# Second-layer sums of one batch: from VectorE adds in SBUF to accumulating transfers into DRAM

## The chip, the cores and the metric

One core of a Trainium2 chip. The metric is the device time of one execution in microseconds; of several runs the median is taken. The core has TensorE (PE: matrix products, with results in PSUM banks), VectorE (DVE), ScalarE (ACT), GpSimd (POOL) and SyncE (SP, which issues most transfers). The engines run side by side, each in its own order, and wait for each other through semaphores.

## The reference

Sigmoid attention, a gated two-matrix block with a shift of one position, and then the block that the change is in. Four batches of S = 448 rows, D = 768 columns, hidden width 3072, all float32. Cut to the part that matters:

```
X = fft(fft(x, axis=1), axis=2)
u = x + real(X)
un = (u - mean(u)) / sqrt(var(u) + 1e-06)
ch = max(un @ w_ch1, 0) @ w_ch2
return u + ch
```

## The kernel before, in words

Every float32 product is done as three PE products of halves: a value is split into `hi` (a rounding cast) and `lo` (the rest), and hi·hi, hi·lo, lo·hi are added in one PSUM bank. A matmul here is 128x128 weights by 448 columns.

The last block keeps `u` transposed in DRAM as `u_d[b]`, six tiles of 128x448 for each batch b. The hidden width is cut into 12 groups g of 256. For batches 0 and 1 `ffn1(g, b)` makes two hidden tiles (18 matmuls each) and `ffn2(g, b)` makes six tiles f2_g_b_e, each of which has to be added to the residual. Batch 0 takes each group by itself (6 matmuls a tile); batch 1 takes g = 0 and g = 1 alone and then two groups at once (12 matmuls a tile), so it has 7 rounds of six tiles. From g = 2 on the order on PE is f1(g,0), f1(g,1), f2(g,0), f1(g+1,0), f1(g+1,1), f2(g+1,0), f2(g+1,1). Batches 2 and 3 come afterwards, in `pair1` and `ffn2(g, 2)`, `ffn2(g, 3)`, with the weights `v2`. Below, f1(g,b) and f2(g,b) are these steps on PE.

The residual sum lives in SBUF: `load_acc(b)` loads `u_d[b]` into a tile `acc[b]` (tag `x2`, three buffers), `out_done` has DVE add each PSUM tile to it, and at the last group the tile goes to `out`. A PSUM bank is free again when its add is done; `bank2` has five of them for these tiles.

Beside this runs `convert`: each weight block w1 or w2 of group g, half i, comes from DRAM as 64-bit numbers (768 KB, by SP) and is turned into float32 on DVE in four steps, then split:

```
yield o.ts(bits, top, 3, 0x3FFFFFF8, ALU.logical_shift_left, ALU.bitwise_and)
yield o.stt(bits, top, 0xC0000000, bits, ALU.bitwise_and, ALU.bitwise_or)
yield o.stt(bits, low, 29, bits, ALU.logical_shift_right, ALU.bitwise_or)
yield o.stt(w, w, TINY, bits.bitcast(F32), ALU.is_ge, ALU.mult)
```

`finish` then has ACT cast `w` to `hi` and POOL subtract it (`lo`, line 215). PE can use the block after that. `prepare_rows` also runs here: DVE and ACT turn batches 2 and 3 into the operands of `pair1`, in a third `x2` tile, `acc2`.

The order of instructions on every engine is written out before the run by the class `Order`: generators such as `convert` and `out_done` yield a time, a planner with a clock of its own (`o.now`, with a cost for each operation) resumes whichever is next, and what it emits becomes the engine's queue. So a change of planned costs moves instructions of other steps against each other.

Of the kernel before, what the change touches and what calls it, by code (L numbers as in the profile page):

```python
# [12 lines left out]
F32 = mybir.dt.float32  # L13
# [3 lines left out]
ALU = mybir.AluOpType  # L17
# [3 lines left out]
B, H, S, DH = 4, 12, 448, 64  # L21
# [4 lines left out]
KD = D // 128  # L26
FF2 = 4 * D
GF = 256
NG = FF2 // GF
# [80 lines left out]
class Order:  # L110
# [126 lines left out]
    def dma(self, out, src, eng=None):  # L237
        (eng or self.nc.sync).dma_start(out, src)
        b = 512 * self.size(out) * (4)
        start = max(self.now + 2.0, self.free.get("dma", 0.0))  # L240
        self.free["dma"] = start + b / 4.0 / 280e3
        return self.free["dma"] + 0.2


def build(tc, ap):
    nc = tc.nc
    V, G = nc.vector, nc.gpsimd
    o = Order(nc)
    est = ExitStack()

    def pool(stack, name, bufs=1, side="left", space=None):
        if space is not None:
            return stack.enter_context(tc.tile_pool(name=name, bufs=bufs, space=space))
        return stack.enter_context(tc.tile_pool(name=name, bufs=bufs, side=side, reuse_waits="tile"))
# [65 lines left out]
    u_d = [dram.tile([128, KD, S], F32, name=f"u_d{b}") for b in range(B)]  # L320
# [182 lines left out]
    for f in range(NF + KD):  # L503
        if f < NF:
            src, hl, key = ap["w_k"][f], [w[:, f].rearrange(flat) for w in (wkh, wkl)], ("wk", f)
        else:
            src, hl, key = ap["w_r"][f - NF], [w.rearrange(flat) for w in wr_t[f - NF]], ("wr", f - NF)
# [148 lines left out]
    np_ = pool(s_r, "norm", 1, "right")  # L656
# [5 lines left out]
    for i, n in enumerate((113, 112, 112, 111)):  # L662
        c = fp.tile([128, 2, TW], F32R, name=f"ct{i}")
# [264 lines left out]
    def load_rs(b, tag):  # L928
        yield from o.need(("rs_d", b))
        rs_t[b] = np_.tile([128, S], F32, tag=tag, name=f"rsb_{b}", bufs=1)  # L930
        o.at["rs", b] = o.dma(rs_t[b], rs_d[b].to_broadcast([128, S]))
# [7 lines left out]
    def load_early(nm, g, pl):  # L939

        ts = w_t[nm, g] = [
            [pl.tile([128, D], F32R, tag=nm + t, name=f"{nm}{t}{g}_{i}", bufs=2) for t in "hl"] for i in range(2)
        ]
        for i in range(2):
            for c, t in enumerate(ts[i]):
                t = o.dma(t.bitcast(F32), w0_d[nm, g][i][:, c])
            o.at.update(((nm, g, i, c), t) for c in range(3))
# [9 lines left out]
    wpa = pool(s_l, "wpa", 2, "left")  # L957
    hp = pool(s_l, "hp", 2, "left")
    wpb1 = pool(s_l, "wpb1", 2, "left")
    acc, h_t = {}, {}  # L960

    def load_acc(b, *keys):

        yield from o.need(*keys, *(("u_d", b, i) for i in range(3)))
        acc[b] = np_.tile([128, KD, S], F32, tag="x2", name=f"acc{b}", bufs=3)
        o.at["acc", b] = o.dma(acc[b], u_d[b])
        yield o.now

    def parts_of(out, src, key, eng):

        yield o.act(out[0], src)
        o.at[key] = t = o.sub(eng, out[1], src, out[0])
        yield t
# [98 lines left out]

    def prepare_rows():

        yield from o.need(*(("centre", b) for b in range(2, B)), ("acc", 1))
        yield from load_rs(2, "rsb")
        yield from load_rs(3, "sum_u")
        wk = np_.tile([128, KD, S], F32, tag="x2", name="acc2", bufs=3)
        yield from o.need(("rs", 2), ("rs", 3))

        def put(nm, d, src):
            if nm not in LATE:
                t = t_t[nm, d] = tp.tile([128, 2, S], F32R, name=f"{nm}_{d}")
                yield from parts_of((t[:, 0], t[:, 1]), src, ("t", nm, d), V)
                return
            t = np_.tile([128, 2, S], F32R, tag="sq", name=f"{nm}_{d}", bufs=1)
            yield from parts_of((t[:, 0], t[:, 1]), src, ("row", nm, d), V)
            o.at["t_d", nm, d] = t = o.dma(t_d[nm, d], t.bitcast(F32))
            yield t + 2.0

        for d in range(3):
            b11, b21, b12, b22 = (wk[:, i] for i in range(4))
            for x, b, e in ((b11, 2, d), (b12, 3, d), (b21, 2, d + 3), (b22, 3, d + 3)):
                yield o.dma(x, c_d[b][:, e])
                yield o.tt(V, x, x, rs_t[b], ALU.mult) + 1.0
            yield from put("B11", d, b11)
            yield o.tt(V, b11, b12, b11, ALU.subtract) + 1.0
            yield from put("T1", d, b11)
            yield o.tt(V, b12, b22, b12, ALU.subtract) + 1.0
            yield from put("T3", d, b12)  # L1100
            yield from put("B22", d, b22)
            yield o.tt(V, b22, b22, b11, ALU.subtract) + 1.0
            yield from put("T2", d, b22)
            yield from put("B21", d, b21)
            yield o.tt(V, b21, b21, b22, ALU.subtract) + 1.0
            yield from put("T4", d, b21)
        acc[2] = wk
        o.at["acc", 2] = o.dma(wk, u_d[2])
# [9 lines left out]
    def hidden(g, b, i, src):  # L1118
# [2 lines left out]
        o.at["h", g, b, i] = o.stt(t[:, 1], src, 0.0, t[:, 0].bitcast(F32), ALU.max, ALU.subtract)  # L1121
        yield o.at["h", g, b, i]

    def out_done(g, b, e, ps):
        yield from o.need(("acc", b))
        a = acc[b][:, e]
        t = o.tt(V, a, a, ps, ALU.add)
        yield t
        if g == NG - 1:
            o.at["out", b, e] = o.dma(ap["out"][e, :, S * b : S * b + S], a) + 2.0  # L1130
            yield o.now

    def network():
# [14 lines left out]
        def ffn2(g, b):  # L1148
            nm = "w2" if b < 2 else "v2"
            gi = [(c, i) for c in ((g - 1, g) if b == 1 and g > 1 else (g,)) for i in range(2)]  # L1150
            yield from o.need(*(("h", c, b, i) for c, i in gi))
            hs = [h_t.pop((c, b, i)) for c, i in gi]
            yield from o.need(*((nm, c, i, 2) for c, i in gi), ("acc", b))
            ws = [w_t[nm, c][i] for c, i in gi]
            for e in range(KD):
                es = slice(128 * e, 128 * e + 128)

                def pair(i, es=es):
                    return ws[i][0][:, es], ws[i][1][:, es], hs[i][:, 0], hs[i][:, 1]

                yield from o.tile(partial(bank2, f"f2_{g}_{b}_{e}"), len(gi), pair, partial(out_done, g, b, e))
            while len(o.feed) > 3:
                yield o.now + 0.1

# [61 lines left out]
        for n, t in enumerate(first):  # L1226
            order.append((ffn2, "w2", t))
            order += [(ffn1, "w1", t) for t in (first + [(2, 0), (2, 1)])[n + 2 : n + 3]]
        for g in range(2, NG, 2):
            order += [(ffn1, "w1", (g, 0)), (ffn1, "w1", (g, 1))] if g > 2 else []  # L1230
            order += [(ffn2, "w2", (g, 0))]
            order += [(ffn1, "w1", (g + 1, 0)), (ffn1, "w1", (g + 1, 1)), (ffn2, "w2", (g + 1, 0)), (ffn2, "w2", (g + 1, 1))]
# [17 lines left out]
    def first_loads():  # L1250
        yield from o.issued(("un", 1, 2))
        load_early("w2", 0, wpa)
        yield from o.issued(("un", 1, 5))
        o.spawn(load_acc(0, ("centre", 1)))
        o.spawn(load_acc(1, ("acc", 0), ("centre", 2)))
        yield o.now + 4.0
        load_early("w1", 1, wpb1)

    o.spawn(first_loads())
    o.spawn(network())  # L1260
    o.run(("four", B - 1))
# [10 lines left out]
    o.spawn(convert())  # L1272
    o.spawn(second_group())
    o.spawn(prepare_rows())
    o.run("converted")
    s_w.close()
# [69 lines left out]
```

## Time and profile before

| | us |
|---|---|
| median of 3 runs | 1229.59 (1227.28 to 1230.06) |
| profiled execution | 1231.31 |
| its span in the trace | 1229.5 |
| PE busy | 1216.5 |
| DVE busy | 907.4 |
| ACT busy | 479.1 |
| POOL busy | 135.3 |

The profiled execution is one run by itself; 1.8 us of its time lie outside the span. Busy times are sums over the span and overlap. The part that the change touches goes from about 562 us (the first f1 and f2) to 896 us (the first `pair1`).

### The profile page before, as it was taken

The page shows a single profiled execution, that of the slowest core. Times are in us where ns is not written, and L with a number is a line of the kernel's source. Part 1 is how long each engine was busy: PE and PEld are TensorE (multiplying, and loading weights), DVE is VectorE, ACT ScalarE, POOL GpSimd, SP SyncE. Part 2 cuts the span into 40 slices and gives each one's busy share as a digit, 9 for nine tenths or more (in the row PEclk, how much of TensorE's full clock was granted, in tenths as well). Part 3 has the DMA queues.
Part 4 walks back from the last instruction along what each step waited for, and adds up shares of the span by engine and source line. Part 5 has one row for each costly group of instructions (what it writes and reads, how often), then busy time and mean ns, then how long its engine had stood idle before and what let it go on. Part 6 is the DMA issues. An engine that isn't in the chain of part 4 may idle for free. (4 is left out here: it accounts for less than half of the span.)

```text
span 1229.5 us, 16416 instructions
## 1 busy us (share of the span) xinstructions
PE 1216.5 (99%) x6142; PEld 1050.5 (85%) x6142; DVE 907.4 (74%) x1425; ACT 479.1 (39%) x864; POOL 135.3 (11%) x97
## 2 busy tenths in 40 slices
PE   8999999999999999999989999999999999999998
PEld 3467766789999998999979999999999999999998
DVE  5776887656853669797999999897566776776654
ACT  5867767766530122142333333332132332322220
POOL 0000000000000000000232232222021111121110
PEclk9999999999999999999999999999999999999999
DMA  6656669666948446396555555555842112121102
GB/s 219 223 169 229 213 239 339 237 243 231 320 158 259 169 165 218 113 316 227 184 202 212 184 200 203 201 186 188 314 141 78 52 54 75 52 66 63 52 1 90
DMA packets 77296, 217.82 MB, mean 177 GB/s; under 512 B 9312, under 2 KB 31776, under 8 KB 76576
## 3 DMA queue, kind: packets, MB, share of 16 engines
q1 hardware_dynamic: 76544, 214.37, 50.3%
q0 software_dynamic: 672, 2.40, 0.6%
q8 instruction: 48, 0.79, 0.3%
q14 instruction: 32, 0.26, 0.1%
HBM read 143.84 MB, written 72.90 MB: 176 GB/s over the span
## 5 line engine op out<-in xcount | busy, mean ns | idle before, releaser
L215 DVE TENSOR_TENSOR acc<-acc,f 128x448 f32<-128x448 f32 x258 | 156.6, 616 | 66.4 <-PE f L180 63.8
L180 PE MATMUL f<-h,w2h 128*128 128x448 f32 x576 | 165.6, 368 | 3.6 <-DVE acc L215 3.6
L180 PE MATMUL f<-un,w1h 128*128 128x448 f32 x576 | 166.2, 368 | 0.0
L180 PE MATMUL f<-h,v2h 128*128 128x448 f32 x576 | 163.6, 365 | 0.0
L180 PEld LDWEIGHTS f<-h,w2h 128*128 128x128 f32 x576 | 107.8, 188 | 14.9 <-DVE acc L215 4.8
L234 ACT ACTIVATE sg<-sc,bias_s 128x448 f32<-128x448 f32 x168 | 95.0, 651 | 60.7 <-PE sc L180 60.7
L180 PEld LDWEIGHTS f<-un,w1h 128*128 128x128 f32 x576 | 108.2, 188 | 10.4 <-issue 0.4
L180 PEld LDWEIGHTS f<-h,v2h 128*128 128x128 f32 x576 | 108.2, 188 | 8.5
L180 PE MATMUL v<-k,wvh 128*128 128x448 f32 x384 | 113.4, 370 | 0.8 <-DMA k<-k_d 0.7
L180 PE MATMUL f<-un,w1l 128*128 128x448 f32 x288 | 105.9, 368 | 0.0
L180 PE MATMUL f<-h,w2l 128*128 128x448 f32 x288 | 105.9, 368 | 0.0
L180 PE MATMUL f<-h,v2l 128*128 128x448 f32 x288 | 105.2, 365 | 0.0
L223 DVE SCALAR_TENSOR_TENSOR w_bits<-w_raw,w_bits 128x768 uint32<-128x768 uint32 x80 | 99.9, 1248 | 1.0
L180 PE MATMUL av<-sg,v 128*64 128x448 f32 (+1 forms) x336 | 81.1, 549 | 0.0
L180 PEld LDWEIGHTS v<-k,wvh 128*128 128x128 f32 x384 | 71.6, 188 | 8.1 <-DMA k<-k_d 2.4
L215 POOL TENSOR_TENSOR v2l<-v,v2h 128x768 fp32r<-128x768 f32 x24 | 46.8, 1970 | 275.0 <-ACT v2h L232 275.0
L215 POOL TENSOR_TENSOR w1l<-w,w1h 128x768 fp32r<-128x768 f32 x20 | 41.2, 2062 | 300.6 <-ACT w1h L232 295.5
L180 PE MATMUL v<-k,wvl 128*128 128x448 f32 x192 | 70.8, 369 | 0.0
L180 PE MATMUL k<-xkh,wkh 128*128 128x448 f32 x192 | 70.7, 368 | 0.0
L180 PE MATMUL k<-xkl,wkh 128*128 128x448 f32 x192 | 70.4, 367 | 0.0
L180 PE MATMUL k<-xkh,wkl 128*128 128x448 f32 x192 | 70.3, 366 | 0.0
L180 PEld LDWEIGHTS av<-sg,v 128*64 128x64 f32 (+1 forms) x336 | 27.9, 144 | 42.5 <-issue 35.9
(175 smaller groups left out, 2356.7 us busy)
## 6 DMA issues: line engine op xcount, KB each, us to landing
w_raw<-in_w SPq DMA_DIRECT2D x40, 768.0 KB, 4.5
w_d<-w SPq DMA_DIRECT2D x40, 384.0 KB, 2.6
k_d<-kp SPq DMA_DIRECT2D x32, 448.0 KB, 2.8
k<-k_d SPq DMA_DIRECT2D x32, 448.0 KB, 6.3
a<-w_d SPq DMA_DIRECT2D x24, 384.0 KB, 3.5
v<-w_d SPq DMA_DIRECT2D x24, 384.0 KB, 3.0
k<-in_k SPq DMA_DIRECT2D x24, 256.0 KB, 5.5
v<-in_v SPq DMA_DIRECT2D x24, 256.0 KB, 3.0
```

The costliest lines, as they stand in the source:

```text
L180: self.nc.tensor.matmul(out, lhs, rhs, start=start, stop=stop, skip_group_check=skip)
L215: eng.tensor_tensor(out, a, c, op=op)
L223: self.nc.vector.scalar_tensor_tensor(out, a, scalar, c, op0=op0, op1=op1)
L234: self.nc.scalar.activation(out, a, fn, **kw)
```

## The change

It concerns batch 1 alone. In place of `acc[1]` there is a tile `stage` of the same size that holds no sums. `out_added` has ACT copy each PSUM tile into `stage[:, e]`; then a transfer issued by GpSimd adds it to `u_d[1][:, e]` in DRAM. After the last group the sum goes from DRAM to `out`, issued by SP. The planner gets a cost for the new step (`add_to`); `prepare_rows` waits for `stage` in the place of `acc[1]`.

```diff
+    def add_to(self, out, src):
+        g = self.nc.gpsimd
+        g.dma_start(out, src, accum_op=ALU.add)
+        t = self.spend(g, 1.2)
+        took = 512 * self.size(out) * 2 / 280e3
+        self.free["dma"] = max(self.now, self.free.get("dma", 0.0)) + took
+        return max(t + 2.0, self.free["dma"]) + took + 0.2
...
     def prepare_rows():
-        yield from o.need(*(("centre", b) for b in range(2, B)), ("acc", 1))
+        yield from o.need(*(("centre", b) for b in range(2, B)), "stage")
...
+    def make_stage():
+        yield from o.need(("acc", 0), ("centre", 2), *(("u_d", 1, i) for i in range(3)))
+        stage[0] = np_.tile([128, KD, S], F32, tag="x2", name="stage", bufs=3)
+        o.at["stage"] = o.now
+        yield o.now
+
+    def out_added(g, e, ps):
+        a = stage[0][:, e]
+        yield o.act(a, ps)
+        o.at["added", g, e] = o.add_to(u_d[1][:, e], a)
+        if g == NG - 1:
+            yield o.at["added", g, e]
+            o.at["out", 1, e] = o.dma(ap["out"][e, :, S : 2 * S], u_d[1][:, e]) + 2.0
+        yield o.now
...
-            yield from o.need(*((nm, c, i, 2) for c, i in gi), ("acc", b))
+            yield from o.need(*((nm, c, i, 2) for c, i in gi), ("acc", b) if b != 1 else "stage")
...
-                yield from o.tile(partial(bank2, f"f2_{g}_{b}_{e}"), len(gi), pair, partial(out_done, g, b, e))
+                done = partial(out_done, g, b, e) if b != 1 else partial(out_added, g, e)
+                yield from o.tile(partial(bank2, f"f2_{g}_{b}_{e}"), len(gi), pair, done)
...
-        o.spawn(load_acc(1, ("acc", 0), ("centre", 2)))
+        o.spawn(make_stage())
```

PE keeps its order of f1 and f2 tiles. On DVE 42 adds go, and what is left stands in another order against PE's tiles. First place: DVE's queue around the conversion of w1_3_1, the weights of the second tile of f1(3,0) and f1(3,1). Before (`f1_2_1_0` is a tile of f1(2,1), `f2_2_0_0` the first of f2(2,0)):

```order
L215 TENSOR_TENSOR acc1_5716<-acc1_5716,f2_1_1_5_6110 128x448
L227 TENSOR_SCALAR w1_3_1_bits_6128<-w1_3_1_raw_6074 128x768
L215 TENSOR_TENSOR acc2_6039<-acc2_6039,rsb_2_5908 128x448
L223 SCALAR_TENSOR_TENSOR w1_3_1_bits_6128<-w1_3_1_raw_6074,w1_3_1_bits_6128 128x768 x2
L223 SCALAR_TENSOR_TENSOR h_2_1_0_6153<-f1_2_1_0_6118,h_2_1_0_6153 128x448
L223 SCALAR_TENSOR_TENSOR w1_3_1_6127<-w1_3_1_6127,w1_3_1_bits_6128 128x768
L227 TENSOR_SCALAR w2_3_0_bits_6182<-w2_3_0_raw_6125 128x768
L223 SCALAR_TENSOR_TENSOR w2_3_0_bits_6182<-w2_3_0_raw_6125,w2_3_0_bits_6182 128x768
L215 TENSOR_TENSOR acc2_6039<-acc2_6039,rsb_3_6037 128x448
L215 TENSOR_TENSOR acc0_5505<-acc0_5505,f2_2_0_0_6186 128x448
```

And in the changed kernel, where `f2_2_0_5` is the last tile of f2(2,0):

```order
L215 TENSOR_TENSOR acc0_5505<-acc0_5505,f2_2_0_3_6199 128x448
L215 TENSOR_TENSOR acc0_5505<-acc0_5505,f2_2_0_4_6210 128x448
L215 TENSOR_TENSOR acc0_5505<-acc0_5505,f2_2_0_5_6218 128x448
L227 TENSOR_SCALAR w1_3_1_bits_6230<-w1_3_1_raw_6149 128x768
L223 SCALAR_TENSOR_TENSOR w1_3_1_bits_6230<-w1_3_1_raw_6149,w1_3_1_bits_6230 128x768
L215 TENSOR_TENSOR acc2_6066<-acc2_6066,rsb_3_6064 128x448
L223 SCALAR_TENSOR_TENSOR w1_3_1_bits_6230<-w1_3_1_raw_6149,w1_3_1_bits_6230 128x768
L223 SCALAR_TENSOR_TENSOR w1_3_1_6229<-w1_3_1_6229,w1_3_1_bits_6230 128x768
L227 TENSOR_SCALAR w2_3_0_bits_6247<-w2_3_0_raw_6227 128x768
L223 SCALAR_TENSOR_TENSOR w2_3_0_bits_6247<-w2_3_0_raw_6227,w2_3_0_bits_6247 128x768
```

The final step of w1_3_1 stood ahead of the add of the first tile of f2(2,0); now the whole conversion stands behind the add of its last tile.

Second place: DVE's queue around w2_4_1, the second half of the weights of f2(4,0) (`f1_4_0` and `f1_4_1` are the tiles of f1(4,0) and f1(4,1), which PE does right before). Before:

```order
L223 SCALAR_TENSOR_TENSOR h_4_0_0_6593<-f1_4_0_0_6557,h_4_0_0_6593 128x448
L227 TENSOR_SCALAR w2_4_1_bits_6613<-w2_4_1_raw_6559 128x768
L223 SCALAR_TENSOR_TENSOR w2_4_1_bits_6613<-w2_4_1_raw_6559,w2_4_1_bits_6613 128x768 x2
L223 SCALAR_TENSOR_TENSOR h_4_0_1_6627<-f1_4_0_1_6590,h_4_0_1_6627 128x448
L223 SCALAR_TENSOR_TENSOR w2_4_1_6612<-w2_4_1_6612,w2_4_1_bits_6613 128x768
L215 TENSOR_TENSOR acc2_6039<-acc2_6039 128x448
L223 SCALAR_TENSOR_TENSOR h_4_1_0_6658<-f1_4_1_0_6625,h_4_1_0_6658 128x448
```

And in the changed kernel:

```order
L223 SCALAR_TENSOR_TENSOR h_4_0_0_6608<-f1_4_0_0_6573,h_4_0_0_6608 128x448
L223 SCALAR_TENSOR_TENSOR w2_4_0_6590<-w2_4_0_6590,w2_4_0_bits_6591 128x768
L223 SCALAR_TENSOR_TENSOR h_4_0_1_6634<-f1_4_0_1_6606,h_4_0_1_6634 128x448
L223 SCALAR_TENSOR_TENSOR h_4_1_0_6659<-f1_4_1_0_6632,h_4_1_0_6659 128x448
L227 TENSOR_SCALAR w2_4_1_bits_6673<-w2_4_1_raw_6588 128x768
L223 SCALAR_TENSOR_TENSOR w2_4_1_bits_6673<-w2_4_1_raw_6588,w2_4_1_bits_6673 128x768 x2
L223 SCALAR_TENSOR_TENSOR h_4_1_1_6687<-f1_4_1_1_6657,h_4_1_1_6687 128x448
L223 SCALAR_TENSOR_TENSOR w2_4_1_6672<-w2_4_1_6672,w2_4_1_bits_6673 128x768
```

The final step of w2_4_1 stood ahead of `h_4_1_0`, the first hidden tile of f1(4,1); now it stands behind `h_4_1_1`, the last one.

Third place: POOL's queue from its `ct` loads on, where before there were only the subtracts (`w1l2_0` is the lo half of w1, g = 2, i = 0). In the changed kernel:

```order
L672 DMA ct3_3908<-in_ct 111x452
L246 DMA u_d1_140<-stage_5716 128x448 x6
L215 ISA
L215 TENSOR_TENSOR w1l2_0_5720<-w1_2_0_5788,w1h2_0_5719 128x768
L215 TENSOR_TENSOR w1l2_1_5722<-w1_2_1_5896,w1h2_1_5721 128x768
L246 DMA u_d1_140<-stage_5716 128x448 x2
L215 TENSOR_TENSOR w2l2_0_5938<-w2_2_0_6027,w2h2_0_5937 128x768
L246 DMA u_d1_140<-stage_5716 128x448 x4
L215 TENSOR_TENSOR w2l2_1_5940<-w2_2_1_6076,w2h2_1_5939 128x768
L215 TENSOR_TENSOR w1l3_0_6119<-w1_3_0_6151,w1h3_0_6118 128x768
L215 TENSOR_TENSOR w1l3_1_6121<-w1_3_1_6229,w1h3_1_6120 128x768
```

The issues of the accumulates stand between the subtracts of the weights, up to six in a row.

## Rows read from the trace of the kernel before

**Rows 1.** The page, part 1: busy time, share of span, instructions.

```profile
PE 1216.5 (99%) x6142; PEld 1050.5 (85%) x6142; DVE 907.4 (74%) x1425; ACT 479.1 (39%) x864; POOL 135.3 (11%) x97
```

**Rows 2.** Waits of PE: total us, times, longest us.

```profile
PE f L180 <- DVE acc L215: 3.6, 2, 2.0
```

**Rows 3.** Timeline of PE: start us, us, what, [idle before <-releaser].

```profile
594.92 0.57 PE L180 MATMUL f<-h,w2h 128*128 128x448 f32 x2
...
609.52 0.57 PE L180 MATMUL f<-h,w2h 128*128 128x448 f32 x2
...
617.73 0.67 PE L180 MATMUL f<-h,w2h 128*128 128x448 f32 x2 [1.97 <-DVE acc L215]
...
619.05 0.56 PE L180 MATMUL f<-un,w1h 128*128 128x448 f32 x2
...
633.63 0.57 PE L180 MATMUL f<-h,w2h 128*128 128x448 f32 x2
...
641.48 0.68 PE L180 MATMUL f<-h,w2h 128*128 128x448 f32 x2 [1.60 <-DVE acc L215]
```

**Rows 4.** Windows: busy us of each engine, granted clock, DMA share, GB/s.

```profile
core 0: us, PE busy (x) PEld busy (x) DVE busy (x) ACT busy (x) POOL busy (x), PEclk, DMA share, GB/s
640.00:900.00 260.00, 258.52 (x1251) 234.79 (x1252) 224.21 (x288) 80.55 (x122) 65.35 (x33) 1.00 0.59 211
600.00:650.00 50.00, 46.43 (x226) 42.04 (x225) 49.67 (x61) 15.01 (x23) 13.90 (x7) 1.00 0.54 192
850.00:900.00 50.00, 50.00 (x245) 45.53 (x244) 26.29 (x42) 10.28 (x18) 5.92 (x4) 1.00 0.66 245
```

**Rows 5.** The chain that ended last: start us, us, what.

```profile
641.48 254.62 PE f L180 x1230
...
956.72 14.60 PE f L180 x72
```

**Rows 6.** Timeline of DVE, 612 to 618 us.

```profile
612.44 0.95 DVE L223 SCALAR_TENSOR_TENSOR w<-w,w_bits 128x768 f32<-128x768 f32 x1
613.43 0.56 DVE L227 TENSOR_SCALAR w_bits<-w_raw 128x768 uint32<-128x768 uint32 x1
614.02 0.96 DVE L223 SCALAR_TENSOR_TENSOR w_bits<-w_raw,w_bits 128x768 uint32<-128x768 uint32 x1
614.90 2.25 DVE L215 TENSOR_TENSOR acc<-acc,rsb 128x448 f32<-128x448 f32 x1
617.07 0.61 DVE L215 TENSOR_TENSOR acc<-acc,f 128x448 f32<-128x448 f32 x1
617.60 0.61 DVE L223 SCALAR_TENSOR_TENSOR h<-f,h 128x448 fp32r<-128x448 f32 x1
```

**Rows 7.** Timelines of ACT and POOL, 599 to 617 us.

```profile
613.43 0.84 ACT L232 CAST w1h<-w 128x768 fp32r<-128x768 f32 x1 [4.94 <-DVE w L223]
...
599.92 1.85 POOL L215 TENSOR_TENSOR w2l<-w,w2h 128x768 fp32r<-128x768 f32 x1 [2.81 <-ACT w2h L232]
...
614.35 2.31 POOL L215 TENSOR_TENSOR w1l<-w,w1h 128x768 fp32r<-128x768 f32 x1 [5.17 <-ACT w1h L232]
```

**Rows 8.** Timelines of PE and DVE at the end of f1(1,1).

```profile
578.70 0.57 PE L180 MATMUL f<-h,w2h 128*128 128x448 f32 x2
...
579.47 0.62 DVE L223 SCALAR_TENSOR_TENSOR h<-f,h 128x448 fp32r<-128x448 f32 x1 [0.71 <-ACT h L234]
```

**Rows 9.** Groups of instructions: shapes, count, busy us, mean ns.

```profile
L232 ACT COPY x<-av 128x448 f32<-128x448 f32 x24 | 12.8, 532 | 6.1 <-issue 3.9 <-PE av L180 2.2
...
L664 POOL DMA_DIRECT2D ct<-in_ct x4 | 2.2, 573 | 0.0
```

**Rows 10.** DMA issues: KB each, median us to landing; the software queue.

```profile
q0 software_dynamic: 672, 2.40, 0.6%
...
w_raw<-in_w SPq DMA_DIRECT2D x40, 768.0 KB, 4.5
...
out<-acc SPq DMA_DIRECT2D x24, 224.0 KB, 2.0
...
cd<-in_cd POOLq DMA_DIRECT2D x1, 1548.0 KB, 13.0
```

More of the change, by code (lines that the diff above doesn't have):

```diff
@@ L959, in build @@
     wpb1 = pool(s_l, "wpb1", 2, "left")
-    acc, h_t = {}, {}
+    acc, h_t, stage = {}, {}, {}
     def load_acc(b, *keys):
```

## The prediction

> **What bounds the kernel now.** I read the page's first part, then what PE waited for, then the chain that ended last, and last the timelines of the few places where PE stopped. PE is busy 1216.5 us of a span of 1229.5, DVE 907.4, ACT 479.1 and POOL 135.3 [rows 1]; so TensorE's own work sets the time, and a change to the other engines counts only where PE is made to wait or is let off a wait. In the part of the program that the change touches PE waited for DVE's `acc` adds twice, 3.6 us together [rows 2]: 1.97 us ahead of the last tiles of f2(2,0) and 1.60 us ahead of the last tile of f2(3,0) [rows 3]. There a PSUM bank was wanted whose tile DVE had not yet added. DVE is the reason: from 600 to 650 us it is busy 49.67 of 50 us [rows 4], so what is queued on it in that stretch comes out late. Near the end of the stage (850 to 900) it has half its time free [rows 4].
>
> PE also has two paces with the same granted clock (1.00 in every window, the 2.4 GHz level [rows 4]). In the chain 1230 matmuls from 641.48 take 254.62 us, 207.0 ns each, and 72 matmuls at 956.72 take 14.60 us, 202.8 ns each [rows 5]. The slow pace began at the wait at 641.48; the stretch to the end of the stage costs 1230 × 4.2 ns = 5.2 us more than the fast pace would. The trace does not say why it began.
>
> **The change, removed.** 42 adds of f2(g,1) leave DVE. In a run of adds one takes 0.53 us start to start (617.07 to 617.60 [rows 6]), so 42 × 0.53 = 22.3 us leave the engine that was full. That removes both waits of [rows 2]: the f2(2,0) one came because six adds of f2(1,1) were done late, and the f2(3,0) one behind the same backlog. Gain 1.97 + 1.60 = 3.57 us. The load of acc1 goes too; nothing waited for it.
>
> **Added, hidden.** 42 ACT copies of 128x448: the like copy takes 532 ns [rows 9], 22.3 us in all, on an engine that is busy 80.55 of 260 us in the stage [rows 4]. 42 DMA issues on POOL: those of `ct` took 573 ns [rows 9], 24.1 us on an engine busy 65.35 of 260 [rows 4]. Cover: at most six issues stand between two subtracts in POOL's order, 3.4 us, and POOL stood idle 2.81 and 5.17 us ahead of its subtracts, waiting for ACT's cast [rows 7]; without that cover each issue would make a subtract 0.57 us later. The transfers: no accumulate of 224 KB stands in the trace. From below, the plain 224 KB store of `out` lands in 2.0 us; from above, the 1548 KB load that POOL issued in 13.0 [rows 10]. I take some 6 us, between them, since it reads and writes DRAM and its issuer is the latter's. A slot of `stage` is used again no earlier than the next f2(g,1), 47 us later for f2(1,1) to f2(3,1) (594.92 to behind 641.48 [rows 3]), so neither bound makes the copy wait. The last step, DRAM to DRAM, starts after 896 us with 330 us of PE work left: nothing. Traffic: 42 × 2 × 0.229 MB = 19.3 MB more; the stage moved 211 GB/s at a DMA share of 0.59 [rows 4], so 100% would be 358 GB/s, and 19.3 MB are 54 us of it over some 330 us, a share of about 0.75 in place of 0.59. The raw weight loads (4.5 us [rows 10]) should stay ahead; the other case is a rival.
>
> **Moved.** The order of DVE is written out again by the planner's clock, and the conversions of three weights now stand later against PE's tiles. The chain behind each final step `w<-w,w_bits` is a cast on ACT and a subtract on POOL: from 612.44 + 0.95 = 613.39 to 614.35 + 2.31 = 616.66, that is 3.27 us, or with the faster subtract of 1.85 us 2.81 [rows 6, 7]. PE wants the subtract's result at the third matmul of a weight.
>
> *w1_3_1.* Before, it ended at 613.39 and its subtract at 616.66, while PE got to f1(3,0) at 619.05 [rows 3, 7]. After, its first conversion step stands behind the last add of f2(2,0). f2(2,0) begins at 609.52 [rows 3], and without its wait its 36 matmuls end at 609.52 + 36 × 0.203 = 616.82. I let the add start 0.2 later, and then follow by the starts of [rows 6] 0.53 (add), 0.59 (613.43 to 614.02), 0.88 (to 614.90), 0.53 (`acc2*rsb`, of the add's size), 0.88 and 0.95 us: 621.4. With 2.81 to 3.27 behind it the subtract ends at 624.2 to 624.7. PE wants it 18 + 2 matmuls after 616.82, at 616.82 + 20 × 0.203 = 620.9. New wait 3.3 to 3.8, taken 3.5. This rests on DVE having caught up with PE here, as it would with 3.2 us less behind it and most of this conversion put off.
>
> *w2_4_1.* Its final step now stands behind the last hidden tile of f1(4,1). The hidden step starts 579.47 − 578.70 = 0.77 us after PE is done [rows 8], 0.53 later the final step of 0.95 begins: 2.25, and with the chain 5.0 to 5.5 us after the end of f1(4,1). PE goes straight on to f2(4,0) and wants it at its sixth matmul, 5 × 0.203 = 1.0 us after. New wait 4.0 to 4.5, taken 4.2.
>
> *w2_10_1.* One hidden tile earlier, so 18 matmuls (3.65 us) better: 0.4 to 0.9, taken 0.6. The others of this kind (w2_6_1, w2_8_1) stand two tiles ahead, as before: nothing.
>
> *Behind w1_3_1* DVE is full again: w2_3_1 comes out between in time and 0.5 us late, and the drain of f2(3,0) may wait for 0 to 1.8 us, the size of the wait it had (1.60). Taken 1.2, the middle of 0 to 2.3.
>
> Sum of new waits: 3.5 + 4.2 + 0.6 + 1.2 = 9.5; less 3.57 is +5.9.
>
> **The pace.** New waits at other places begin the two paces anew. Bounds: 0 and −5.2 for the slow stretch. In the trace a wait was followed by either pace (fast after 617.73: 72 matmuls from 619.05 to 633.63, 14.58 us [rows 3]; slow after 641.48), so I take half, −2.6. Net +3.3. On the profiled execution's own 1231.31 (span 1229.5 and 1.8 around it) that is 1234.6; this execution was 1.72 above the median of the three, so the forecast for the median is 1232.9, said as 1233.0.
>
> A page speaks against the transfers being free. The Trainium skill, "DMA: Bandwidth & Descriptors", section "Issuing engines are not separate DMA queues", says that DMAs started by any engine run on the same 16 DMA engines and interleave. By that the second rival below would be the likely one; whether the trace agrees it cannot show, since POOL's five DMAs, 0.6% of the share, lie apart from this stage.
>
> **Rivals.**
> 1. *The relief wins; faster.* The two waits go, and the moved conversions are not late, because PE is itself held up somewhere ahead or because DVE reaches those steps sooner. It is decided at w1_3_1: its subtract must end before 620.9. Then −3.57, and with the pace −3.57 to −8.8: 1226 to 1221 for the median. For it: DVE has 22 us less to do. Against it: the order is fixed, and both final steps stand behind tiles of PE.
> 2. *Loads late.* The accumulates slow the 768 KB raw loads. They come in bursts of six within 14.6 us, when the share is already 0.59 on average. If a load takes 9 us in place of 4.5, and about half of that shows at the four places where PE comes straight from f1 to f2 (g = 4, 6, 8, 10), that is 4 × 2.2 = 9 us above the forecast: 1242. Against it: two raw buffers, each load issued a conversion ahead, and two conversions took 14.4 us (599.92 to 614.35 [rows 7]).
> 3. *One for one.* The new waits come to half of what I count, since each of the two has parts of slack that I don't see: 4 us against 3.57: 1229.6 to 1230, no change.
> 4. *Accumulates far slower than bounded.* At 13 us each and one behind another, six take 78 us, and the copies of f2(3,1) would find their slots of `stage` 31 us late (47 us after the use before), PE with them for want of banks: over 1260. Against it: the plain store's 2.0 us [rows 10], and that transfers overlap.
>
> **How the numbers follow.** 0.2%, 2.46 us, is about what a measurement of this kernel can tell from no change: same is 1227.1 to 1232.05. The likeliest case, chance 0.56, has its own range from 7.6 − 5.2 − 3.57 = −1.2 to 11.4 − 3.57 = +7.8: 1228.4 to 1237.4 (0.42 slower, 0.14 same). Rival 1 has 0.18 (0.16 faster, 0.02 same), rival 2 0.12 (slower), rival 3 0.12 (0.10 same, 0.02 faster), rival 4 0.02. Together faster 0.18, same 0.26, slower 0.56. The range 1225.0 to 1240.5 leaves out most of rival 1's lower part and the worse half of rival 2.
>
> **What would show it.** Right: the waits on DVE acc are gone at f2(2,0); PE waits on POOL's `w1l` in f1(3,0) for about 3.5 us and on ACT's `w2h` or POOL's `w2l` at the start of f2(4,0) for about 4.2; ACT's copies and POOL's issues near 0.53 and 0.57 us; DMAs `u_d<-stage` landing in 2 to 13 us; pace after 641 at or below 207 ns. Wrong: no wait at those two places; waits of the conversions' first step on DMA raw loads (rival 2); ACT copies waiting on DMA (rival 4); a pace that changes also outside this stage.

## The result, and the profile after

The changed kernel is slower: 1236.82 us median of 5 runs (1236.08 to 1241.87) against 1227.28 for the kernel before (1225.60 to 1230.06, 5 runs), a ratio of 1.0081, 95% interval 1.0055 to 1.0107. The profiled execution took 1236.3 us with a span of 1234.5. The forecast was 1233.0 with a range of 1225.0 to 1240.5 and slower as the likeliest sign: sign and range held, and the likeliest case's own range (1228.4 to 1237.4) too, but +9.5 us was measured where +3.4 to the median was forecast.

From the page of the changed kernel: busy times, the software queue, the group of POOL's issues, and the landing time of the new transfers.

```profile
PE 1217.1 (99%) x6142; PEld 1054.0 (85%) x6142; DVE 883.7 (72%) x1383; ACT 499.4 (40%) x906; POOL 169.3 (14%) x139
...
q0 software_dynamic: 6720, 12.03, 5.6%
...
L246 POOL DMA_DIRECT2D u_d<-stage x42 | 37.2, 1038 | 238.5 <-ACT stage L232 236.9
...
u_d<-stage POOLq DMA_DIRECT2D x42, 224.0 KB, 6.7
```

DVE has 23.7 us less work than in [rows 1], ACT 20.3 more. An accumulate lands in 6.7 us (forecast 6). POOL is busy 0.89 us in each issue (37.2 / 42; the 1038 ns of the row is a mean over records that overlap), not 0.57. The software queue's transfers take 5.6% of 16 engines' span against 0.6% [rows 10]: 69.1 − 7.4 = 61.7 us, 1.47 us of the 16 engines for each accumulate.

What PE waited for after (total us, times, longest us), in the place of [rows 2]:

```profile
PE f L180 <- ACT w2h L232: 2.4, 1, 2.4
PE f L180 <- ACT w1h L232: 1.8, 1, 1.8
PE f L180 <- POOL w1l L215: 1.7, 1, 1.7
PE f L180 <- POOL w2l L215: 1.3, 2, 1.1
```

The two waits on `acc` are gone. In their place PE waits for ACT's cast and POOL's subtract of two weights. The PE timeline at both places, f1(3,0) and f2(4,0), each with the first matmul of the step, the waits, and the first matmul of the step after:

```profile
616.81 0.57 PE L180 MATMUL f<-un,w1h 128*128 128x448 f32 x2
...
622.47 0.68 PE L180 MATMUL f<-un,w1h 128*128 128x448 f32 x2 [1.84 <-ACT w1h L232]
624.85 0.74 PE L180 MATMUL f<-un,w1l 128*128 128x448 f32 x1 [1.71 <-POOL w1l L215]
625.39 0.95 PE L180 MATMUL f<-un,w1h 128*128 128x448 f32 x2
...
629.87 0.71 PE L180 MATMUL f<-un,w1h 128*128 128x448 f32 x2
...
637.92 0.57 PE L180 MATMUL f<-h,w2h 128*128 128x448 f32 x2
...
674.40 0.57 PE L180 MATMUL f<-h,w2h 128*128 128x448 f32 x2
...
677.58 0.83 PE L180 MATMUL f<-h,w2h 128*128 128x448 f32 x2 [2.41 <-ACT w2h L232]
679.48 0.74 PE L180 MATMUL f<-h,w2l 128*128 128x448 f32 x1 [1.06 <-POOL w2l L215]
...
688.27 0.57 PE L180 MATMUL f<-un,w1h 128*128 128x448 f32 x2
```

f1(3,0) and f1(3,1) together take 637.92 − 616.81 = 21.11 us where the same 72 matmuls took 14.58 before [rows 3]. The third matmul of the late weight starts at 624.85; 20 matmuls at 0.203 behind 616.81 it would have been 620.87, so it is 3.98 us late (1.84 + 1.71 us of them idle in the rows, the rest around the two matmuls between). That leaves 6.53 − 3.98 = 2.55 us. f2(4,0) takes 688.27 − 674.40 = 13.87 us where 36 matmuls at 0.203 are 7.30, 6.57 us more; its sixth matmul starts at 679.48 in place of 675.41, 4.07 us late, which leaves 2.50. The rest is TensorE's clock. From 625.39 to 629.87 twelve matmuls take 373 ns each, against 203 before the wait. The windows (columns as in [rows 4]) show the granted clock:

```profile
620.00:640.00 20.00, 16.45 (x69) 14.40 (x68) 19.68 (x22) 7.80 (x12) 6.48 (x3) 0.83 0.56 190
...
625.00:630.00 5.00, 5.00 (x14) 4.45 (x15) 4.88 (x6) 2.53 (x4) 1.86 (x1) 0.50 0.69 244
...
672.00:680.00 8.00, 4.52 (x19) 3.40 (x18) 7.32 (x9) 2.94 (x5) 1.81 (x1) 0.87 0.43 153
680.00:690.00 10.00, 10.00 (x40) 9.13 (x39) 9.28 (x14) 1.64 (x2) 1.84 (x1) 0.76 0.59 219
690.00:900.00 210.00, 209.72 (x1035) 194.01 (x1034) 170.08 (x207) 76.19 (x122) 69.30 (x49) 1.00 0.74 233
```

It is below 1.00 in the windows at and behind the waits, 0.50 from 625 to 630 us, which is the lower level, 1.2 GHz, and 1.00 from 690 us on. The long matmuls last for some 5 us at each place. From 624.85 to 629.87 PE does 13 matmuls, which at 203 ns would take 2.64 us: that is 2.4 of the 2.55. The Trainium skill, "TensorE: Matmul & The Clock Gate", section "What's actually happening", says that a gate sets the clock by how busy PE has recently been and knows two levels, 1.2 and 2.4 GHz. The durations here agree: there are two of them, and the longer begin behind PE's waits.

The chain that was late, first on DVE (for w1_3_1 and then for w2_4_1):

```profile
617.01 0.62 DVE L215 TENSOR_TENSOR acc<-acc,f 128x448 f32<-128x448 f32 x1 [0.59 <-PE f L180]
...
620.59 0.96 DVE L223 SCALAR_TENSOR_TENSOR w<-w,w_bits 128x768 f32<-128x768 f32 x1
...
675.17 0.62 DVE L223 SCALAR_TENSOR_TENSOR h<-f,h 128x448 fp32r<-128x448 f32 x1 [0.57 <-ACT h L234]
675.72 0.95 DVE L223 SCALAR_TENSOR_TENSOR w<-w,w_bits 128x768 f32<-128x768 f32 x1
```

and then on ACT and POOL:

```profile
621.58 0.83 ACT L232 CAST w1h<-w 128x768 fp32r<-128x768 f32 x1 [7.47 <-DVE w L223]
...
676.70 0.83 ACT L232 CAST w2h<-w 128x768 fp32r<-128x768 f32 x1 [1.56 <-DVE w L223]
...
622.49 2.30 POOL L215 TENSOR_TENSOR w1l<-w,w1h 128x768 fp32r<-128x768 f32 x1 [7.28 <-ACT w1h L232]
```

The last add of f2(2,0) starts at 617.01, the final step of w1_3_1 ends at 621.55 (forecast 621.4), the subtract at 624.79 (forecast 624.2 to 624.7). The final step of w2_4_1 follows the last hidden tile, 675.17, as the order said.

### The profile page after: what moved, and what is told of

Same layout as the page of the kernel before. It is cut to its first block, busy times and chain, and to the rows that moved or that the text cites. A ratio compares the mean times of both kernels' runs of the same rounds, so it can differ in the third digit from the quotient of the medians.

```text
span 1234.5 us, 16529 instructions
## 1 busy us (share of the span) xinstructions
PE 1217.1 (99%) x6142; PEld 1054.0 (85%) x6142; DVE 883.7 (72%) x1383; ACT 499.4 (40%) x906; POOL 169.3 (14%) x139
## 4 chain that ended last, share of the span: by engine, by line
PE 82%; issue 10%; POOL 5%; DMA 1%; ACT 0%; DVE 0%; SPq 0%; POOLq 0%; ACTq 0%
PE f L180 29%; PE k L180 10%; PE v L180 9%; PE r L180 7%; PE sc L180 6%; PE av L180 6%; PE f_X L180 4%; PE f_W L180 4%; PE f_Z L180 3%; POOL w2l L215 2%; POOL w1l L215 2%; PE f_Y L180 2%; POOL u_d L246 1%; PE pq L180 1%; DMA k<-k_d 1%
## 5 line engine op out<-in xcount | busy, mean ns | idle before, releaser
L215 DVE TENSOR_TENSOR acc<-acc,f 128x448 f32<-128x448 f32 x216 | 131.6, 617 | 55.4 <-PE f L180 52.5
L180 PEld LDWEIGHTS f<-h,w2h 128*128 128x128 f32 x576 | 109.6, 190 | 11.5 <-ACT w2h L232 2.8
L246 POOL DMA_DIRECT2D u_d<-stage x42 | 37.2, 1038 | 238.5 <-ACT stage L232 236.9
```

The source lines that it names most:

```text
L180: self.nc.tensor.matmul(out, lhs, rhs, start=start, stop=stop, skip_group_check=skip)
L215: eng.tensor_tensor(out, a, c, op=op)
L246: g.dma_start(out, src, accum_op=ALU.add)
```

## The experiments

The theory after the result, called the order theory: the loss is that two conversions stand later in DVE's order, so that PE waits twice and twice goes on at the lower clock; the planner put them there because it books 1.64 us of DMA time for each accumulate, and plans the raw loads behind that. Rivals: the traffic of the accumulates itself makes the loads late (traffic theory), or POOL's longer issues delay the subtracts (issue theory). The order theory allows a test from both sides, since the booking is a number of the planner and changes no instruction. Each ratio below is against the kernel before, run beside that experiment (medians 1226.29 to 1226.82 us).

**after_nobook.** The changed kernel, nothing booked:

```diff
-        took = 512 * self.size(out) * 2 / 280e3
+        took = 0.0
```

The conversion of w1_3_1 then ends ahead of `h_2_1_0` (before: behind it), that of w2_4_1 ahead of `h_4_1_0`, as before.

> The changed kernel with one planner number changed: an accumulate books no DMA time in the planner (0 in place of 1.64 us). The instructions are the same, the transfers on the chip too; the planner only puts the conversions of w1_3_1 and w2_4_1 ahead of their hidden tiles again. Order theory (the late places of these two conversions cost the time): PE waits for w1h, w1l, w2h, w2l gone, clock 1.00 throughout, and the gain of the removed DVE adds is left: 1227.3 less 3.9 us, 1222 to 1225. Traffic theory (the accumulates delay the raw loads, and the planner was right to book them): DVE now waits on the raw loads in order, PE waits about as before, 1234 to 1238. Issue theory (POOL's issues of 1.04 us delay the subtracts): waits on POOL stay, 1230 to 1236.

1223.58 us (1221.40 to 1225.67, 8 runs), ratio 0.9971 (0.9957 to 0.9984): faster than the kernel before by 3.2 us, and by 13 us than the changed kernel. PE waits for no weight; of `f` one wait is left:

```profile
PE f L180 <- DVE acc L215: 0.6, 1, 0.6
```

The gain forecast from the waits removed, 3.9 us with the gap around them, less this 0.6 is 3.3. The order theory holds. But the traffic is real: DVE waits for raw loads now,

```profile
DVE w_bits L227 <- DMA w_raw<-in_w: 11.5, 7, 2.8
```

seven times, 11.5 us together. An early place with a wait of DVE for the data cost PE no wait for a weight, where a late place cost it one.

**before_book.** The other side: the kernel before, DVE's adds and no accumulate, with the booking alone:

```diff
         t = o.tt(V, a, a, ps, ALU.add)
+        if b == 1:
+            o.free["dma"] = max(o.now, o.free.get("dma", 0.0)) + 512 * o.size(a) * 2 / 280e3
         yield t
```

> The kernel before, its adds on DVE and no accumulate, with one line more in the planner: each add of batch 1 books the DMA time that the change's accumulate books. That moves the conversions of w1_3_1 and w2_4_1 behind f2(2,0)'s last add and behind h_4_1_1, as in the changed kernel. Order theory: slower like the changed kernel and worse, since DVE's adds remain: two waits of 3.5 us or more, each followed by a stretch at the lower clock that costs 2.6 us, 1227.3 + 12 = 1239, from 1236 to 1245. Traffic theory or issue theory: no accumulate is there, so no change, 1225.5 to 1230.

1241.73 us (1237.53 to 1244.66, 6 runs), ratio 1.0113 (1.0092 to 1.0134). With no accumulate in it, the order alone makes the kernel slower by 14.9 us in the median (three runs are near 1244, three between 1237.5 and 1239.6). The longest waits of PE for weights (another of 1.1 us is for `acc`, in f2(3,0)):

```profile
PE f L180 <- ACT w2h L232: 3.6, 1, 3.6
PE f L180 <- POOL w1l L215: 3.4, 2, 1.7
PE f L180 <- POOL w2l L215: 1.2, 1, 1.2
```

The windows at the first of the `w1l` waits, at f2(4,0), and after it:

```profile
588.00:600.00 12.00, 10.29 (x51) 9.00 (x50) 9.38 (x17) 3.60 (x6) 2.49 (x2) 1.00 0.58 187
672.00:690.00 18.00, 13.16 (x51) 11.28 (x51) 16.26 (x20) 6.03 (x9) 5.01 (x3) 0.81 0.67 232
690.00:890.00 200.00, 200.00 (x970) 181.63 (x969) 171.52 (x219) 61.63 (x92) 48.95 (x25) 1.00 0.57 200
```

f2(4,0) came as expected (3.6 + 1.2 us and a clock of 0.81), f1(3,0) otherwise: there its wait was 0.39 + 1.70 us, another of 1.71 stands in f1(2,0), and neither was followed by the lower clock. Here the waits of 1.71 and 1.70 us left the clock at 1.00, and that of 3.6 did not. The order at f1(3,0) is not quite that of the changed kernel: the first step of w1_3_1 stands ahead of the last two adds of f2(2,0) (618.47), and only its final step (622.49) behind the last. The profiled execution (1244.19) also had the slow pace behind it, 970 matmuls in 200 us.

**no_transfer.** The changed kernel, its order kept, without the transfers, so that the sums of batch 1 are left out:

```diff
-        g.dma_start(out, src, accum_op=ALU.add)
```

> The changed kernel without its 42 accumulating transfers: ScalarE's copies stay, the sums of batch 1 are left out, and the order of all other instructions is as in the changed kernel. Order theory: PE's waits at f1(3,0) and f2(4,0) and the two stretches at the lower clock stay, 1235 to 1238. Traffic theory and issue theory: most of the loss goes, 1223 to 1230.

1235.79 us (1233.76 to 1238.44, 4 runs), ratio 1.0073 (1.0056 to 1.0090). The same four waits on `w1h`, `w1l`, `w2h`, `w2l` (1.8, 1.7, 2.4, 1.1 us) and both stretches at the lower clock: taking all traffic away gave back 1 us of 9.5 at most. Most of that lies in the stretch at the lower clock: f1(3,0) and f1(3,1) take 20.25 us here (616.42 to 636.67) in place of 21.11, with the same waits. Traffic and issues are not the cause of the loss.

**filled.** The changed kernel with matmuls in the place of the two waits:

```diff
+    def filled(get, n, lhs, rhs):
+        ps = get()
+        for _ in range(n):
+            o.mm(ps[:, 0:S], lhs, rhs, True, True, cost=1e-9, skip=True)
+        return ps
...
+                if (g, b, i) == (3, 0, 1):
+                    get = partial(filled, get, 20, w_t["w1", 3][0][0][:, 0:128], un_t[0, 0][:, 0])
...
+                if (g, b, e) == (4, 0, 0):
+                    get = partial(filled, get, 19, ws[0][0][:, es], hs[0][:, 0])
```

> The changed kernel with 20 matmuls more ahead of the second tile of f1(3,0) and 19 more ahead of the first tile of f2(4,0), into the bank that the tile then overwrites; they fill the two waits (4.0 and 3.9 us) and no other instruction moves. If the clock fell because PE stood idle there: no wait, no stretch at the lower clock, 2 x 2.6 us less than the changed kernel, 1236.8 - 5.2 + 0.1 = 1231.7, from 1230.5 to 1233. If the clock falls for another reason at these places (the DMA traffic, the engines' load): both stretches stay, 1236 to 1238. If the added matmuls only delay: above 1240.

1233.58 us (1231.66 to 1235.37, 6 runs), ratio 1.0054 (1.0041 to 1.0067). The clock stayed at 1.00 in both places (windows):

```profile
615.00:640.00 25.00, 24.95 (x122) 22.42 (x121) 23.46 (x28) 7.61 (x12) 6.56 (x4) 1.00 0.54 185
672.00:690.00 18.00, 17.90 (x88) 16.27 (x88) 17.29 (x22) 5.17 (x8) 3.71 (x2) 1.00 0.57 202
```

So it was PE's standing still that lowered it, since all other work was as before. The gain was 3.2 us and not 5.1. PE now waits for `acc` again,

```profile
PE f L180 <- DVE acc L215: 1.3, 2, 0.8
```

at 644.16 and about 707 us, where in the changed kernel the slow stretches had given DVE time to catch up. The other 0.6 us are within the spread of the runs (1231.66 to 1235.37).

**late_w1 and late_w2.** One late place each, by booking only some rounds (`g < 2`, and `0 < g < 4`):

```diff
-        took = 512 * self.size(out) * 2 / 280e3
+        took = 512 * self.size(out) * 2 / 280e3 if booked else 0.0
...
-        o.at["added", g, e] = o.add_to(u_d[1][:, e], a)
+        o.at["added", g, e] = o.add_to(u_d[1][:, e], a, g < 2)
```

> The changed kernel, with DMA time booked in the planner for the accumulates of f2(0,1) and f2(1,1) alone: w1_3_1 stands late (behind the last add of f2(2,0)) as in the changed kernel, w2_4_1 early. Order theory, each late place costing by itself: 1223.6 (nothing late) + one wait of 3.5 to 4.0 us + 2.6 us of lower clock = 1230, from 1228.5 to 1231.5, one stretch at the lower clock, in f1(3,0). If the places help each other (a first wait makes the second): near 1236.8 or near 1223.6.

1232.99 us (1230.55 to 1234.46, 5 runs), ratio 1.0046 (1.0030 to 1.0062), more than expected. f1(3,0) is as in the changed kernel (1.8 and 1.7 us, and the lower clock). But PE also waits in f2(4,0):

```profile
PE f L180 <- POOL w2l L215: 1.5, 1, 1.5
PE f L180 <- ACT w2h L232: 0.5, 1, 0.5
```

This happened though w2_4_1 stands early: DVE waited for its raw load until 667.30, 8.3 us after SP had issued it. The lower clock followed here too: from 676.07 to 678.31 six matmuls take 373 ns each.

> The changed kernel, with DMA time booked for the accumulates of f2(1,1) and f2(3,1) alone: w2_4_1 stands late (behind h_4_1_1) as in the changed kernel, w1_3_1 early. Order theory: 1223.6 + 3.5 + 2.6 = 1230, from 1228.5 to 1231.5, one stretch at the lower clock, in f2(4,0). If the places help each other: near 1236.8 or near 1223.6.

1235.63 us (1233.92 to 1236.86, 4 runs), ratio 1.0063 (1.0043 to 1.0083), again more than expected. At f2(4,0) PE did this:

```profile
668.35 0.56 PE L180 MATMUL f<-h,w2h 128*128 128x448 f32 x2
...
674.57 1.12 PE L180 MATMUL f<-h,w2h 128*128 128x448 f32 x2 [5.46 <-ACT w2h L232]
676.96 0.74 PE L180 MATMUL f<-h,w2l 128*128 128x448 f32 x1 [1.27 <-POOL w2l L215]
...
685.69 0.57 PE L180 MATMUL f<-un,w1h 128*128 128x448 f32 x2
```

6.7 us of waits in place of 3.5. DVE's timeline shows why, and that the expectation was worked out from the wrong rows:

```profile
669.12 0.62 DVE L223 SCALAR_TENSOR_TENSOR h<-f,h 128x448 fp32r<-128x448 f32 x1 [0.31 <-ACT h L234]
669.66 0.55 DVE L227 TENSOR_SCALAR w_bits<-w_raw 128x768 uint32<-128x768 uint32 x1
```

In this order the whole conversion stands behind the last hidden tile (its first step at 669.66), and not its final step alone. With the lower clock behind it that place costs 10.0 us (685.69 − 668.35 = 17.34 where 36 matmuls at 0.203 are 7.31), and this execution had the slow pace behind it, 206.7 ns a matmul to the end of the stage. So late_w2 is no test of the changed kernel's own second place. Each place makes PE wait by itself; that the two together cost the sum of the parts is not shown, since neither kernel repeats one place alone as it was.

**late_w1_no_transfer.** late_w1 without the transfers, to see whether the accumulates had made its second wait.

> The kernel with w1_3_1 late alone, without its 42 accumulating transfers (the sums of batch 1 are left out), same order. With them it took 1233.0 and PE waited in f2(4,0) too (0.54 + 1.52 us and a stretch at the lower clock), although w2_4_1 stood early; its raw load had come late. If the accumulates delayed that load: the waits in f2(4,0) go, the waits in f1(3,0) (1.8 + 1.7 us) and one stretch at the lower clock stay, 1228 to 1230. If the order alone made that wait too: unchanged, 1232 to 1234.

1230.74 us (1229.43 to 1236.39, 10 runs), ratio 1.0034 (1.0019 to 1.0049), 2.2 us below late_w1, though the two intervals overlap. Waits of PE:

```profile
PE f L180 <- POOL w2l L215: 1.2, 1, 1.2
```

Between the two expectations: `w2h`'s wait went, `w2l`'s fell from 1.5 to 1.2 us, and no lower clock followed it. By these two executions the accumulates made part of that wait and the order the rest.

**nobook_no_transfer.** after_nobook without the transfers.

> The changed kernel with nothing booked, and without its 42 accumulating transfers (the sums of batch 1 are left out): ScalarE's copies and the early conversions alone. If the transfers and their issues cost nothing behind PE's work: as with them, 1222.5 to 1224.7. If the bursts cost something (slow raw loads, late subtracts, the pace of 207 ns): lower by that, 1218 to 1222.

1221.80 us (1221.39 to 1222.94, 5 runs), ratio 0.9957 (0.9943 to 0.9971), 1.8 us below after_nobook. The landing times of the raw loads (minimum, median, maximum, us) with the transfers and without:

```profile
DMA to landing us min/median/max: 4.4/5.0/14.2
```

```profile
DMA to landing us min/median/max: 4.3/4.7/8.6
```

The slowest load takes 14.2 us beside the bursts and 8.6 without them, where before it was 8.7. So the transfers cost 1.0 to 1.8 us (against nobook_again, below, and after_nobook) of the 4.8 that the change gave without them (1226.62 − 1221.80). 0.6 is the wait on `acc` at 637.39, absent here; ahead of it DVE had waited 2.62 us for a raw load, at 609.65. What the rest is, the pace included, is not shown. The Trainium skill, "DMA: Bandwidth & Descriptors", section "Issuing engines are not separate DMA queues", says that transfers of all engines interleave on one set of 16 DMA engines. These landing times agree.

**before_again and nobook_again.** Second profiles of two kernels, unchanged, for the pace.

> The kernel before, unchanged, profiled once more for the pace of PE between 641 and 896 us. If the slow pace (207 ns) belongs to this kernel: the same stretch slow again. If it belongs to one execution: another stretch, or none, and the time lower than 1231.3 by 4 ns for each matmul that went at the fast pace, down to 1225.6.

> The changed kernel with nothing booked, once more, for a second profile and its time beside the former: 1222 to 1225.5. If the slow pace of its first profile (690 to 890 us at 206 to 207 ns in part) belongs to the execution, it lies elsewhere or is absent here; if it belongs to the kernel, it is at the same place.

before_again took 1225.68 us. Its PE timeline at the wait on `acc` in f2(2,0), and the window there:

```profile
616.56 0.93 PE L180 MATMUL f<-h,w2h 128*128 128x448 f32 x2 [1.99 <-DVE acc L215]
...
617.66 0.95 PE L180 MATMUL f<-h,w2h 128*128 128x448 f32 x2
...
619.90 0.72 PE L180 MATMUL f<-un,w1h 128*128 128x448 f32 x2
620.45 0.37 PE L180 MATMUL f<-un,w1l 128*128 128x448 f32 x1
```

```profile
616.00:620.00 4.00, 3.44 (x10) 3.07 (x11) 4.00 (x7) 0.14 (x1) 0.00 (x0) 0.60 0.32 126
```

The same place, a wait of 1.99 us in place of 1.97, and here the clock fell behind it (matmuls of 373 ns up to 619.90). The second wait on `acc`, 1.60 us in the first profile, is absent in this one. The slow pace lay at 621 to 645 us and not from 641 to 896. nobook_again took 1222.83 us (1221.83 to 1225.20, 10 runs), ratio 0.9971 (0.9960 to 0.9982). The window from 750 to 890 us in the first and in the second profile of this one kernel:

```profile
750.00:890.00 140.00, 140.00 (x680) 127.14 (x679) 102.05 (x131) 47.78 (x78) 44.41 (x33) 1.00 0.77 239
```

```profile
750.00:890.00 140.00, 140.00 (x693) 129.64 (x693) 102.47 (x131) 48.33 (x80) 46.10 (x34) 1.00 0.78 244
```

680 matmuls against 693 in the same 140 us, with a granted clock of 1.00 in both. The slow pace belongs to the execution and not to the kernel's code.

## Why the prediction was right, and where its sum was off

- *Both waits on DVE go, 3.57 us.* Right: they are absent after, and with the conversions in their early places the kernel gains 3.2 us.
- *ACT's copies, POOL's issues, the transfers: hidden.* Right in the sum: the issues and transfers are within 1 us (no_transfer), though an issue takes 0.89 us and not 0.57, and the copies take 533 ns (forecast 532). Hidden does not mean free: in after_nobook issues and transfers cost 1.0 to 1.8 us, in part through late loads.
- *w1_3_1, 3.5 us late.* Measured 3.98. *w2_4_1, 4.2 us.* Measured 4.07. *w2_10_1, 0.6 us.* Measured 0.28. *Behind w1_3_1, 1.2 us.* Measured nothing; PE's stretch at the lower clock gave DVE the time (without that stretch, in filled, PE waits 0.8 us there). New waits 8.3 us in place of 9.5.
- What failed is the step "The pace", and a term that the sum lacks. The prediction took −2.6 us for a change of pace. The pace belongs to the execution: the kernel before showed its slow stretch at two different places in two profiles, and its times spread from 1225.1 to 1230.6. The profiled execution, from which the sum started, was above all of them. Against the median that term should have been nothing.
- The missing term is the price behind a wait. At both places PE went on at the lower clock, 2.5 us each. Put right, the sum is 6.5 + 6.6 (both places) + 0.3 (f2(10,0)) − 3.9 (both waits on `acc`, with the gaps around them: 617.73 and 641.48 less 30 matmuls at 0.203 behind 609.52 and 633.63 [rows 3], 2.1 + 1.8) = +9.5, and +9.5 was measured. That they agree to 0.1 is luck, since the measured interval is +6.8 to +13.1. Two traces without a long slow pace give +8.9 for the stage itself: from f2(1,1) to the first `pair1` the changed kernel takes 305.6 us (594.93 to 900.57), before_again 296.7 (593.73 to 890.46). The trace of before shows no lower clock behind its waits of 1.97 and 1.60 us, and I read it as if a wait cost only itself.
- That the likeliest case's own range held is in part luck too. The forecast stood on a median before of 1229.59; beside the changed kernel it was 1227.28. The measured +9.5 on 1229.59 would have been 1239.1, above 1237.4.
- The bounds of the new waits add up to 7.7 and 11.5, not 7.6 and 11.4; nothing hangs on it.
- Rival 2, the late loads, had its mechanism right in part: the slowest raw load lands in 13.7 us after, 8.7 before, but the median in 4.9 and not in 9 (4.5 before). With an early place in the order that is covered but for the price above.

## What to carry to other kernels

Where a planner writes the order, a number that it books for a new step can cost more than the step: look first at what moved against the bottleneck engine, and try the step with its booking at nothing. An early place in an engine's order, with a wait for the data, may cost nothing where a late place costs the engine that is waited for. On a TensorE that is never idle, price a new wait with the clock that may follow it: here PE was 4 us late at each of two places, and each cost 6.5 us, or 5.7 at the first one where the stretch at the lower clock was shorter (no_transfer).

## What was not expected of the hardware

A wait near 2 us on TensorE was followed by the lower clock in one execution (1.99 us) and not in another (1.97 us) of the same kernel at the same place, and waits of 1.70 and 1.71 us (before_book) were not; waits of 0.54 and 1.52 us with two matmuls between them (late_w1) were. Behind the same waits at f1(3,0) the stretch at the lower clock cost 2.55 us in the changed kernel and 1.7 in no_transfer. Why the pace of matmuls changes between 203 and 207 ns at an unchanged granted clock, for some 20 to 250 us at a time, stays open; these runs show only that it differs between executions of the same kernel.
